# First batch of a block-sparse attention and feed-forward kernel: value products with turned probabilities as 32-column stationary tiles, outputs normalised after the product and then turned, first loads in another order

## The chip, the core and the metric

The kernel runs on one core of a Trainium2 chip. TensorE (PE) multiplies matrices; it holds a stationary operand that is loaded by its own instruction (PEld in the profile) and streams a moving operand through it. VectorE (DVE), ScalarE (ACT) and GpSimd (POOL) do elementwise work, and the DMA queues are fed by the SP and ACT instruction streams. The metric is the device time of one execution, in microseconds (us), lower is better.

## The reference, cut to what matters

```python
# batch 4, heads 8, sequence 768, head size 64; blocks of 32 rows, 24 blocks
scores = q @ k.T / 8
mask = |block_i - block_j| <= 1, or block 0 or 23 on either side, or one of 3 sampled blocks
scores = where(mask, scores, -1e9); scores -= max(scores)
attn = exp(scores); attn = attn / (sum(attn) + 1e-9)
x = (attn @ v)            # laid out as 3072 tokens x 512
out = ((x @ w_a) * (x @ w_b)) @ w_out    # 512 -> 1536 -> 512, float32 results
```

A query block of 32 rows (a "unit" below) reads all 768 keys if it is block 0 or 23 (a dense unit) and 8 blocks, 256 keys, otherwise (a sparse unit).

## The kernel before, in words

The program is written by generators that ask a planner (`Plan`) for time on an engine. The planner holds an assumed duration for every step (`pe(1050, ...)`, `dve(420, ...)`), picks the next step greedily by its assumed start, with a weight times the step's rank added on DVE, SP and the loads, and so fixes the order of the instructions on every engine before anything runs. On the chip each engine then works its list off in order, with semaphore waits between engines. So a change of an assumed duration or of a rank can change the order everywhere.

Work goes by chunks of 256 query rows (8 units), 12 chunks in all. The first batch has the chunks 0, 1 and 2, taken in the order 1, 0, 2: chunk 1 is eight sparse units, chunk 0 is one dense and seven sparse, chunk 2 seven sparse and one dense. Batches 1 to 3 are computed with operands split in two 16-bit parts; the first batch ("plain") is computed in float32, since the splitting machinery is not running yet, and since the three feed-forward weight matrices have to be unpacked and split in the same time (`weights`, lines L751 to L801: load, three DVE passes, an ACT pass for the bound, and the split on ACT and DVE, 36 pieces).

A sparse unit of the first batch goes: POOL collects the keys (`gather_keys`, L603 to L608); PE writes the duplicate mask (L971) and adds the scores (`plain_scores`, L820: four heads, each 32 stationary columns of queries, into four 32-row strips of PSUM); DVE takes the maximum (L986); ACT does exp with the sum (L999) into `sm`; DVE takes the reciprocal (L1006); `plain_norm` multiplies `sm` by it, once for each of two groups of four heads (L924 on DVE or L927 on ACT); `plain_turn` transposes the four 128-column pieces on PE (L940) and copies them from PSUM (L947 or L948) to `pt`; then `values_into` multiplies by the values (L878). There the stationary operand is 128 columns of values (two heads of 64) and the moving operand is 64 columns of `pt` (two heads of 32 queries), so the result `av` comes with head and feature on the partitions, as the feed-forward part wants it. Of the product of two heads by two heads, half is used. When two units are done, `output` writes `xT` in two 16-bit parts from each half of the partitions (`output_half`, L1210 on ACT and L1211 on DVE, 64 partitions by 256, twice).

A dense unit does the same in four quarter steps (two groups of heads, two halves of the keys) with 384 keys each, and has one normalisation and three transposes for each.

`first_products` (L1246) multiplies `xT` by the weights, one of 12 slices of the 1536 at a time, when a chunk's `xT` and that slice's weights are there; `second_products` (L1334 to L1336) does the other matrix. The PSUM ring `ab` (two buffers) serves both L1246 and the transposes L940.

At the start the ACT queue issues the four key loads, then the first value load, a query load, three value loads, a query load, the three small tables (sampled blocks twice, block constants) with the 128x128 identity (`eye`, which borrows a buffer of the ring `hl`), and then the weights. A load is planned on an engine of its own (`LOAD`) though ACT issues it. The mask rows (`mrows`, 8 blocks by 32 equal columns) and the offsets of the sampled blocks are computed on DVE from the small tables. The values are loaded at the start only to find their bound (L532, `v_scale`), which `output` needs; the products read them by their own loads (`gather_values`, L638 to L654, on SP).

Of the kernel before, what the change touches and what calls it, by code (L numbers as in the profile page):

```python
# [9 lines left out]
BF16 = mybir.dt.bfloat16  # L10
# [8 lines left out]
NB = 24  # L19
# [36 lines left out]
W_PE, W_DVE, W_ACT, W_POOL, W_SP = 0, 1, 0, 0, 2  # L56
SLACK = 0
R_NOW, R_P2, R_P1 = -50, 8000, 9000

# [173 lines left out]
def load_way(moved, fn):  # L233

    return [Way("LOAD", 475, fn, moved)]

# [6 lines left out]
def kernel(  # L243
# [96 lines left out]
    v_stored = [Event(NG) for _ in range(B)]  # L340
    q_ready = [Event(3 if cc >= NCH else 2) for cc in range(NC)]
    tables = Event()
    eye_ready = Event()
    eye, eye_used = [None], Event(NB - 2 + 4 * HQ)
    mask_ready = Event()
# [42 lines left out]


    def make_tables():  # L390

        box = work.tile([P, DM], F32, tag="st", name="mbox", bufs=ST_BUFS)
        held = yield from take("st", ST_BUFS)
        row = work.tile([P, DM], F32, tag="st", name="mrow", bufs=ST_BUFS)
        rings.setdefault("hl", Ring(HL_BUFS)).freed.append(eye_used)
        whole = work.tile([P, 2 * HQ * NK // 2], F32, tag="hl", name="eye", bufs=HL_BUFS)
        eye[0] = whole[:, :P]
        held2 = yield from take("st", ST_BUFS)
# [9 lines left out]
        def load():  # L408
            nc.scalar.dma_start(
                one.rearrange("p a b -> p (a b)"),  # L410
                sampled_blocks.bitcast(I32).rearrange("(o a) b -> o (a b)", o=1),
            )
            nc.scalar.dma_start(
                sb.rearrange("p a b -> p (a b)"), sampled_blocks.bitcast(I32)
            )
            nc.scalar.dma_start(cb, c_blocks)
            nc.scalar.dma_start(eye[0], c_eye)

        t = yield [Way("ACT", 300, load, 500)]
        eye_ready.fire(t)  # L420

# [15 lines left out]
        def doubles():  # L437
            nc.vector.tensor_copy(sv[:, 0:5], cb[:, 0:5])
            nc.vector.tensor_scalar(
                sv[:, 5:8], sb[:, :, 0], 0.0, float(NB - 1), ALU.max, ALU.min  # L440
            )
            nc.vector.memset(ident, 0.0)
            nc.vector.memset(mrows, 0.0)
            nc.vector.tensor_copy(ident[:NB], cb[:, 5 : 5 + NB])
            nc.vector.memset(dup, 0.0)
            for s in range(3, 8):
                nc.vector.tensor_scalar(
                    eq[:, :s], sv[:, :s], sv[:, s : s + 1], MASKED, ALU.is_equal, ALU.mult
                )
# [3 lines left out]
            nc.vector.tensor_copy(mrows[:NB], dup.unsqueeze(2).to_broadcast([NB, 8, BLK]))  # L453

# [25 lines left out]
    def keys(b, g):  # L480
        if b == 0:
            t = yield load_way(1000, lambda: nc.scalar.dma_start(plain_keys[:, g], k[0, g]))
            k_ready[0].fire(t)
            if g + 1 < NG:
                plan.start(keys(0, g + 1), -LEAD_K)
            return
# [33 lines left out]
    def values(b, g):  # L520
# [194 lines left out]
    def plain_queries(cc, u0):  # L715

        q_used[cc] = yield from take("QT", QT_BUFS)
        t = work.tile([P, 2, NG, CH], F32, tag="QT", name=f"QZ{cc}", bufs=QT_BUFS)
        QT[cc] = t
        parts_of = [slice(0, D), slice(D, P)]  # L720

        def blank():
            for y in range(2):
                nc.gpsimd.memset(t[parts_of[1 - y], y], 0.0)

        end = yield pool(1800, blank)
# [132 lines left out]
    def values_into(b, i, quads, first, last):  # L859


        if i % 2 == 0 and quads[0][0] == 0 and first:
            av_ev[0] = yield from take("av", 2)
            av_ps[0] = psum.tile([P, NG, 2, 64], F32, tag="av", name=f"av{b}_{i}", bufs=2)
        av = av_ps[0]

        def pair_sums(g, terms):
            cols = slice((g % 2) * 64, (g % 2) * 64 + 64)
            each = []
            for pt, hi, lo, vals in terms:  # L870
                if lo is None:
                    each.append((vals[:, g % 2 * P : g % 2 * P + P], pt, hi))
                    continue
                v0 = g % 2 * 4 * D
# [14 lines left out]

        each = 240 if b == 0 else 180  # L890
        t = yield pe(sum(len(terms) for _, terms in quads) * each + 80, sums)
        if last and quads[-1][0] == HQ - 1:
# [28 lines left out]

    def plain_norm(sm, over, n):
        return [
            Way("DVE", 150 + n * 0.53, lambda: nc.vector.tensor_scalar(  # L924
                sm, sm, over, None, ALU.mult
            )),
            Way("ACT", 290 + n * 0.83, lambda: nc.scalar.activation(  # L927
                sm, sm, AF.Copy, scale=over
            )),
        ]  # L930

    def plain_turn(sm, pt, name, freed):
# [5 lines left out]
        def turns_():  # L938
            for x in range(cols):
                nc.tensor.transpose(ps[:, x], sm[:, x * P : (x + 1) * P], eye[0])  # L940

        t = yield pe(110 * cols, turns_)
        freed.fire(t)
        eye_used.fire(t)
        n = cols * P
# [7 lines left out]
    def attend(b, i):  # L953
# [27 lines left out]

        t = yield pe(1050 if b == 0 else 850, all_scores)
        kg_free[kn].fire(t)
# [20 lines left out]
        if b == 0:  # L1004
# [3 lines left out]
            mine.fire(0)  # L1008
            for hq in range(HQ):
                yield plain_norm(sm[:, hq], den[:, at, hq, 0:1], NK)  # L1010
            mine = yield from turn("pt", b, i)
# [8 lines left out]
                (hq, [  # L1020
                    (pt, 2 * hq + x, None, vg[:, x, hq * 4 * D : (hq + 1) * 4 * D])
                    for x in range(2)
# [54 lines left out]
    def attend_quad(b, i, hq, ends):  # L1077
# [17 lines left out]
        for x in range(2):  # L1095
            t = yield pe(700 if b == 0 else 450, lambda x=x: half_scores(x))
        if hq == 0:
# [63 lines left out]
    def all_values(b, i, hq, x, pt, kept):  # L1161
# [6 lines left out]
        if b == 0:  # L1168
            vg = plain_vg(m).rearrange("p a x -> p (a x)")
            terms = [(pt, y, None, vg[:, y * 4 * D : (y + 1) * 4 * D]) for y in range(3)]  # L1170
        else:
# [14 lines left out]
    def output(b, i, av, read):  # L1186
# [3 lines left out]
        if p >= 2:  # L1190
            yield ffn_done[seq[p - 2]]
        if b == 0:
            yield v_scale[0]
        t0 = i % PER * BLK
        left = Event(2)
        for half in range(2):
# [5 lines left out]
            lo4 = lo.rearrange("p g (i x) -> p g i x", i=2)  # L1202
            plan.start(output_half(cc, half, of, hi4, lo4, left, read), order[b, i] - LEAD_X)
        yield from ()

    def output_half(cc, half, of, hi, lo, left, read):
        s = float(2.0 ** -14)
        if cc < NCH:
            s = scale[half * 64 : half * 64 + 64, at_v : at_v + 1]
        yield act(380, lambda: nc.scalar.activation(hi, of, AF.Copy, scale=s))  # L1210
# [182 lines left out]
def _laid_out(name, a):  # L1393
# [11 lines left out]
    elif name in ("k", "v"):  # L1405

        B, H, S, _ = a.shape
        first = a[0].transpose((0, 2, 1) if name == "k" else (1, 0, 2))
        a = a.reshape(B, H // 2, 2, S // P, P, D)
# [37 lines left out]
```

## Time and profile before

| | |
|---|---|
| median of 3 runs | 929.02 us (922.42 to 936.56) |
| the profiled execution's own time | 930.45 us |
| its span, first to last instruction | 928.7 us |
| busy: PE, DVE, ACT, POOL | 835.5, 549.9, 435.8, 169.3 us |
| mean granted clock of TensorE in it | 0.969 of full speed |

The trace is of the one profiled execution, so sums are made against its 930.45 us. A float32 matmul of the first batch stands in the trace as two records (two passes), a transpose as one. Busy shares are of a stretch; PEclk is the granted clock as a share of 2.4 GHz. First-batch attention runs from about 21 to 262 us of the span.

### The profile page before, as it was taken

What the parts mean: (1) busy time and instruction counts of PE and PEld (TensorE: products, weight loads), DVE (VectorE), ACT (ScalarE), POOL (GpSimd) and SP (SyncE); (2) the same over time, 40 slices, a digit from 0 to 9 for tenths busy, and PEclk for the clock granted to TensorE, in tenths of its full rate; (3) what the DMA queues carried; (4) which work ended last, traced back from release to release, by engine and by line L of the source; (5) the groups of instructions that cost most, each with busy time, mean ns of one, the idle gap of its engine ahead of it and who ended that gap; (6) DMA issues with size and microseconds to landing.
All of it is one profiled execution on the core that took longest, in us unless ns stands there. A gap on an engine that the chain in (4) does not pass through costs nothing.

```text
span 928.7 us, 23488 instructions
## 1 busy us (share of the span) xinstructions
PE 835.5 (90%) x8912; PEld 669.1 (72%) x8912; DVE 549.9 (59%) x1527; ACT 435.8 (47%) x1074; POOL 169.3 (18%) x415
## 2 busy tenths in 40 slices
PE   0788987899998787989999999999989999999998
PEld 0466865678876665777777777778777787788886
DVE  1778898966567665555666665645675625332222
ACT  2455655666546475543465564434655424232222
POOL 3431313112033331100332220001421300000000
PEclk9777997999999998999999999999999999999999
DMA  8655684397577599974686985627755506442000
GB/s 258 211 161 185 185 256 138 123 187 207 141 167 169 136 224 168 191 152 95 161 153 164 225 170 154 144 68 167 164 127 139 115 13 145 94 96 48 24 1 23
DMA packets 173083, 133.48 MB, mean 144 GB/s; under 512 B 116841, under 2 KB 141546, under 8 KB 172394
## 3 DMA queue, kind: packets, MB, share of 16 engines
q1 hardware_dynamic: 161760, 94.15, 45.1%
q10 hardware_dynamic: 11210, 37.82, 13.4%
q8 instruction: 70, 1.15, 0.5%
q14 instruction: 43, 0.35, 0.1%
HBM read 87.89 MB, written 12.58 MB: 108 GB/s over the span
## 4 chain that ended last, share of the span: by engine, by line
PE 52%; DMA 18%; DVE 15%; ACT 6%; SPq 5%; issue 3%; ACTq 0%; POOL 0%; POOLq 0%; DVEq 0%
PE ab L1246 24%; DMA pt<-hl 10%; PE av L878 8%; PE o L1334 5%; PE o L1336 4%; PE o L1335 4%; DMA keysT<-ks 2%; DVE hl L854 2%; PE s L820 2%; ACT sm L999 2%; DVE xT L1211 2%; SPq L652 2%; PE tp L940 2%; DVE hl L850 2%; ACT xT L1210 1%
## 5 line engine op out<-in xcount | busy, mean ns | idle before, releaser
L1246 PE MATMUL ab<-xT,wab 128*128 128x256 f16 x3456 | 407.3, 275 | 3.6 <-DVE a L1281 2.8
L1246 PEld LDWEIGHTS <-wab 128*128 128x128 f16 x3456 | 330.9, 99 | 73.6 <-issue 34.0
L878 PE MATMUL av<-pt,VG 128*128 128x64 f16 (+1 forms) x2464 | 138.0, 212 | 22.1 <-DMA VG<-vd 15.6
L1334 PE MATMUL o<-woh,gh 128*128 128x512 f32 x288 | 126.5, 439 | 10.0 <-ACT gh L1303 8.8
L1281 DVE TENSOR_TENSOR a<-a,ab 128x256 f32<-128x256 f32 x144 | 59.9, 416 | 124.7 <-ACT a L1278 123.7
L1278 ACT ACTIVATE a<-ab,f 128x256 f32<-128x256 f32 x144 | 67.8, 471 | 126.0 <-PE ab L1246 120.7
L1336 PE MATMUL o<-woh,gl 128*128 128x512 f32 x288 | 114.9, 399 | 1.2 <-DVE gl L1306 1.0
L603 POOL COPY KG<-keysT 128x384 int32<-128x384 int32 (+1 forms) x88 | 52.0, 591 | 347.2 <-PE s L829 240.3
L1335 PE MATMUL o<-wol,gh 128*128 128x512 f32 x288 | 113.1, 393 | 0.0
L999 ACT ACTIVATE sm<-s,low,cq 128x256 f32<-128x256 f32 x132 | 73.6, 561 | 65.0 <-DVE hl L854 33.1
L608 POOL COPY KG<-keysT 128x128 int32 (+1 forms) x264 | 91.8, 385 | 40.7 <-POOL KG L603 26.0
L878 PEld LDWEIGHTS <-VG 128*128 128x128 f16 x2016 | 69.3, 98 | 34.7 <-issue 23.5
L1303 ACT CAST gh<-a 128x256 fp32r<-128x256 f32 x132 | 53.2, 403 | 84.9 <-DVE a L1281 83.4
L850 DVE TENSOR_SCALAR hl<-sm,den 128x256 f16<-128x256 f32 (+1 forms) x117 | 43.6, 374 | 66.4 <-DMA pt<-hl 66.3
L854 DVE SCALAR_TENSOR_TENSOR hl<-sm,den,hl 128x256 f16<-128x256 f32 (+1 forms) x156 | 78.8, 513 | 6.2 <-ACT hl L847 4.6
L1306 DVE TENSOR_TENSOR gl<-a,gh 128x256 fp32r<-128x256 f32 x132 | 57.9, 439 | 35.0 <-ACT gh L1303 33.3
L1334 PEld LDWEIGHTS o<-woh,gh 128*128 128x128 f32 x288 | 54.6, 190 | 28.4 <-ACT gh L1303 11.4
L1336 PEld LDWEIGHTS o<-woh,gl 128*128 128x128 f32 x288 | 54.3, 188 | 17.3 <-DVE gl L1306 5.0
L878 PEld LDWEIGHTS av<-pt,VG 128*128 128x128 f32 x448 | 59.9, 213 | 7.5 <-DVE pt L948 2.9
L986 DVE TENSOR_REDUCE low<-s 128x2 f32<-128x512 f32 x88 | 59.9, 681 | 7.6 <-PE s L820 5.6
L971 PE MATMUL s<-mrows,ident 128*32 128x192 bf16 (+1 forms) x352 | 25.1, 274 | 43.6 <-ACT sm L999 21.8
L1335 PEld LDWEIGHTS o<-wol,gh 128*128 128x128 f32 x288 | 54.8, 190 | 6.7
(109 smaller groups left out, 827.6 us busy)
## 6 DMA issues: line engine op xcount, KB each, us to landing
VG<-vd SPq DMA_DIRECT2D x210, 64.0 KB, 2.1
VG<-vd SPq DMA_DIRECT2D x66, 192.0 KB, 2.9
VG<-vd SPq DMA_DIRECT2D x24, 384.0 KB, 3.6
out_dram<-ou SPq DMA_DIRECT2D x24, 256.0 KB, 2.4
VG<-in_v_dram SPq DMA_DIRECT2D x74, 64.0 KB, 2.8
q<-in_q_dram ACTq DMA_DIRECT2D x9, 512.0 KB, 5.2
stage<-in_k_dram ACTq DMA_DIRECT2D x12, 384.0 KB, 4.3
QT<-QT SPq DMA_DIRECT2D x18, 256.0 KB, 3.7
```

The lines of the kernel that those rows point to most:

```text
L608: nc.gpsimd.tensor_copy(to[:, :, (5 + r) * w : (6 + r) * w], of[:, :, bass.ds(at, w)])
L850: Way("DVE", 227 + n * 0.49, lambda: nc.vector.tensor_scalar(hi, sm, over, None, ALU.mult), 0, X_HIGH),
L854: t = yield dve(221 + n * 1.03, lambda: nc.vector.scalar_tensor_tensor(lo, sm, over, hi, ALU.mult, ALU.subtract))
L878: mm(av[:, g, i % 2, :], w, pt[:, y, cols], start=(i % 2 == 0 and g == 0 and first and n == 0), stop=(last and n == len(each) - 1), skip_g ...
L986: yield dve(685, lambda: nc.vector.tensor_reduce(mx, ps, axis=mybir.AxisListType.X, op=ALU.max, negate=True))
L999: t = yield act(750, lambda hq=hq: nc.scalar.activation(sm[:, hq], ps[:, hq], AF.Exp, bias=low[:, at, hq, 0:1], scale=factor_of(b, cc, hq) ...
L1246: mm(ab[:, i, :], wab[:, f, i, part, kt, :], xc[:, kt, a, :], start=(i == 0 and kt == 0 and part + a == 0), stop=(kt == KT - 1 and a == 1) ...
L1278: yield act(470, lambda: nc.scalar.activation(a_sb, ab[:, 0, :], AF.Copy, scale=fb[:, f : f + 1]))
L1281: t = yield dve(420, lambda: nc.vector.tensor_mul(a_sb, a_sb, ab[:, 1, :]))
L1334: mm(po, gh[:, js], woh[:, f, :], start=(f == 0), stop=False)
L1335: mm(po, gh[:, js], wol[:, f, :], start=False, stop=False)
L1336: mm(po, gl[:, js], woh[:, f, :], start=False, stop=(f == NF - 1))
```

## The change

For the first batch, the value product has the turned probabilities of one head as stationary operand (32 columns) and the head's 64 value columns as moving operand; four heads go to four 32-row strips of PSUM, as the scores do. The probabilities are turned without being normalised. After each pair of units the product is multiplied by the reciprocal sums on DVE (`xs`), turned back by two PE transposes into a buffer of the ring `ab`, and the two parts of `xT` are written from all 128 partitions at once. Heads are grouped by even and odd for that, with the value layout, the key indices and the query indices arranged to fit.

At the start the tables and the query loads go through SP, the four key loads are started together with ranks ahead of everything else on ACT, the identity has its own buffer and load, the bound's value loads get a later rank, and the value gathers of the first batch wait for the keys. Loads are planned on ACT. `mrows` is held as 8 columns, and the mask matmul reads each of them 32 times (step 0). The planner's assumed durations of the first batch's PE steps change.

```diff
+PLAIN_S, PLAIN_T, PLAIN_AV = 430, 215, 240
...
-    return [Way("LOAD", 475, fn, moved)]
+    return [Way("ACT", 475, fn, moved)]
...
-    mrows = const.tile([P, 8, BLK], BF16, name="mrows")
+    mrows = const.tile([P, 8], BF16, name="mrows")
+    eye = const.tile([P, P], F32, name="eye")
...
+    def load_eye():
+        t = yield load_way(300, lambda: nc.scalar.dma_start(eye, c_eye))
+        eye_ready.fire(t)
...
-        t = yield [Way("ACT", 300, load, 500)]
-        eye_ready.fire(t)
+        yield [Way("SP", 1300, load, 250, 1)]
+        plan.start(load_eye(), -20)
...
-            plan.start(values(b, g + 1), order[b, 0] - LEAD_V)
+            plan.start(values(b, g + 1), order[b, 0] - (LEAD_V if b else 1))
...
-        if b > 0:
-            yield v_stored[b]
+        yield v_stored[b] if b > 0 else k_ready[0]
...
-            end = yield load_way(700, lambda y=y: nc.scalar.dma_start(
+            end = yield sp(650, 700, lambda y=y: nc.sync.dma_start(
...
-            g, y = divmod(4 * hq + h, 2)
             mm(
-                to[h * BLK : (h + 1) * BLK], QT[cc][:, y, g, r : r + BLK], rhs(g),
+                to[h * BLK : (h + 1) * BLK], QT[cc][:, hq, h, r : r + BLK], rhs(h),
...
+        def plain_sums():
+            for hq, terms in quads:
+                for n, (pt, y, vals) in enumerate(terms):
+                    for h in range(4):
+                        mm(
+                            av[h * BLK : (h + 1) * BLK, i % 2, hq, :],
+                            pt[:, y, h * BLK : (h + 1) * BLK], vals[:, h * D : (h + 1) * D],
+                            start=(i % 2 == 0 and hq == 0 and first and n == 0),
+                            stop=(last and n == len(terms) - 1), skip_group_check=True,
+                        )
...
-    def plain_norm(sm, over, n):
...
-                    mrows[:, lo:].rearrange("p s x -> p (s x)").unsqueeze(1).to_broadcast(
-                        [P, HQ, NK - lo * BLK]
+                    mrows[:, lo:].unsqueeze(1).unsqueeze(3).to_broadcast(
+                        [P, HQ, 8 - lo, BLK]
...
-            for hq in range(HQ):
-                yield plain_norm(sm[:, hq], den[:, at, hq, 0:1], NK)
...
-                yield plain_norm(sms[x], d1, HALF)
...
+    def plain_output(i, av, read, to, cc):
+
+        at = order[0, i] % LATE
+        held = yield from take("hl", HL_BUFS)
+        xs = work.tile([P, 2, HQ, D], F32, tag="hl", name=f"xs{i}", bufs=HL_BUFS)
+        over = den[:, at : at + 2, :, 0].unsqueeze(3).to_broadcast([P, 2, HQ, D])
+        t = yield dve(418, lambda: nc.vector.tensor_mul(xs, av, over))
+        read.fire(t)
+        freed = yield from take("ab", 2)
+        ps = psum.tile([P, NG, 2, BLK], F32, tag="ab", name=f"tx{i}", bufs=2)
+
+        def turns_():
+            for x in range(2):
+                nc.tensor.transpose(
+                    ps[:, :, x], xs[:, x].rearrange("p a d -> p (a d)"), eye
+                )
+
+        t = yield pe(2 * PLAIN_T, turns_)
+        held.fire(t)
+        yield v_scale[0]
+        s = scale[:, at_v : at_v + 1]
+        of = ps.rearrange("p g i x -> p g (i x)")
+        hi, lo = to[:, :, 0], to[:, :, 1]
+        yield act(470, lambda: nc.scalar.activation(hi, of, AF.Copy, scale=s))
+        t = yield dve(420, lambda: nc.vector.scalar_tensor_tensor(
+            lo, of, s, hi, ALU.mult, ALU.subtract
+        ))
+        freed.fire(t)
...
-        plan.start(keys(0, 0), -LEAD_K)
-        plan.start(queries(seq[0]), -LEAD_Q)
-        plan.start(make_tables(), 0)
-        plan.start(values(0, 0), -LEAD_V)
+        for g in range(NG):
+            plan.start(keys(0, g), -29 + g)
+        plan.start(queries(seq[0]), -30)
+        plan.start(make_tables(), -40)
+        plan.start(values(0, 0), -1)
```

## Rows read from the trace of the kernel before

**Rows 1.** Busy us by stretch: PE, PEld, DVE, ACT, POOL, PEclk, DMA share, GB/s:

```profile
0.00:20.00 20.00, 0.00 (x0) 0.10 (x1) 2.33 (x17) 5.12 (x10) 7.64 (x21) 1.00 0.85 257
20.00:80.00 60.00, 44.79 (x351) 32.31 (x354) 44.23 (x122) 27.04 (x73) 18.71 (x38) 0.74 0.64 199
80.00:200.00 120.00, 105.05 (x915) 82.80 (x907) 102.96 (x279) 71.78 (x174) 27.98 (x58) 0.93 0.58 172
200.00:265.00 65.00, 64.59 (x597) 53.12 (x594) 38.12 (x99) 35.06 (x80) 9.16 (x22) 1.00 0.67 174
```

**Rows 2.** The chain that ended last, 20 to 80 and 80 to 200 us:

```profile
by line: PE av L878 31.0%; PE s L820 15.2%; PE tp L940 11.5%; DMA stage<-in_moe_w_b_dram 10.9%; ACT xT L1210 5.3%; DVE xT L1211 4.9%; DVE wab L770 3.7%; DVE wab L773 3.3%; ACT sm L999 2.4%; PE s L971 2.3%; DVE low L986 2.2%; ACT sm L927 1.9
...
by line: PE ab L1246 15.1%; PE av L878 13.6%; DMA keysT<-ks 8.3%; PE s L820 5.7%; DVE w L770 4.7%; DVE w L773 4.5%; PE tp L940 3.9%; DVE wab L795 3.0%; ACT xT L1210 2.8%; issue 2.8%; DMA VG<-in_v_dram 2.6%; DVE low L986 2.5%; DVE w L767 2.4
```

**Rows 3.** Timeline of the first 32 us: start, duration, what:

```profile
8.73 0.50 POOL L603 COPY KG<-keysT 128x384 f32<-128x384 f32 x1 [4.07 <-DMA keysT<-in_k_dram]
...
11.06 0.69 ACTq L409 DMA_DIRECT2D mrow<-in_sampled_blocks_dram  x1
...
15.60 0.18 DVE L423 TENSOR_SCALAR mrow<-mrow 1x72 f32<-1x72 int32 x1 [14.64 <-DMA mrow<-in_sampled_blocks_dram]
...
17.18 0.77 POOL L608 COPY KG<-keysT 128x128 f32 x3 [7.47 <-issue]
...
18.24 0.19 DVE L438 COPY mbox<-mbox 24x5 f32<-24x5 f32 x1
...
21.51 0.35 PE L971 MATMUL s<-mrows,ident 128*32 128x192 bf16 x4 [21.51 <-DVE mrows L453]
...
23.69 0.43 DVE L767 TENSOR_SCALAR wab<-stage 128x512 int32<-128x512 int32 x1 [1.90 <-DMA stage<-in_moe_w_b_dram]
```

**Rows 4.** Busy time by stretch of the value products (L878) alone, PE and PEld:

```profile
20.00:80.00 60.00, 21.13 (x128) 20.39 (x128) 0.74 0.64 199
80.00:200.00 120.00, 23.14 (x176) 22.43 (x176) 0.93 0.58 172
200.00:265.00 65.00, 17.96 (x162) 17.75 (x162) 1.00 0.67 174
```

**Rows 5.** PE timeline: start, duration, what:

```profile
35.42 3.68 PE L878 MATMUL av<-pt,VG 128*128 128x64 f32 x16
38.89 1.91 PE L940 MATMUL tp<-eye,sm 128*128 128x128 f32 x8
...
103.53 0.49 PE L940 MATMUL tp<-eye,sm 128*128 128x128 f32 x3
103.95 0.27 PE L971 MATMUL s<-mrows,ident 128*32 128x192 bf16 x4
104.04 1.04 PE L820 MATMUL s<-KG,QZ 128*32 128x256 f32 x16
105.01 1.55 PE L878 MATMUL av<-pt,VG 128*128 128x64 f32 x12
...
108.23 1.89 PE L878 MATMUL av<-pt,VG 128*128 128x64 f32 x16
109.96 0.61 PE L940 MATMUL tp<-eye,sm 128*128 128x128 f32 x4
110.49 0.27 PE L971 MATMUL s<-mrows,ident 128*32 128x192 bf16 x4
```

**Rows 6.** The chain that ended last, 120 to 310 us, a 16-bit score group:

```profile
282.95 0.44 PE s L829 x16
```

**Rows 7.** Groups by form: busy us and mean ns, then idle before:

```profile
L1281 DVE TENSOR_TENSOR a<-a,ab 128x256 f32<-128x256 f32 x144 | 59.9, 416 | 124.7 <-ACT a L1278 123.7
...
L1211 DVE SCALAR_TENSOR_TENSOR xT<-av,scale,xT 64x256 f16<-64x256 f32 x24 | 11.6, 482 | 19.3 <-ACT xT L1210 19.0
```

**Rows 8.** Busy time by stretch of the normalisations on DVE (L924):

```profile
20.00:80.00 60.00, 5.06 (x14) 0.74 0.64 199
80.00:200.00 120.00, 5.17 (x15) 0.93 0.58 172
```

More of the change, by code (lines that the diff above doesn't have):

```diff
@@ L340 @@
     v_stored = [Event(NG) for _ in range(B)]
-    q_ready = [Event(3 if cc >= NCH else 2) for cc in range(NC)]
+    q_ready = [Event(3) for _ in range(NC)]
     tables = Event()
     eye_ready = Event()
-    eye, eye_used = [None], Event(NB - 2 + 4 * HQ)
     mask_ready = Event()
@@ L394, in make_tables @@
         row = work.tile([P, DM], F32, tag="st", name="mrow", bufs=ST_BUFS)
-        rings.setdefault("hl", Ring(HL_BUFS)).freed.append(eye_used)
-        whole = work.tile([P, 2 * HQ * NK // 2], F32, tag="hl", name="eye", bufs=HL_BUFS)
-        eye[0] = whole[:, :P]
         held2 = yield from take("st", ST_BUFS)
@@ L408, in load @@
         def load():
-            nc.scalar.dma_start(
+            nc.sync.dma_start(
                 one.rearrange("p a b -> p (a b)"),
@@ L452, in doubles @@
                 )
-            nc.vector.tensor_copy(mrows[:NB], dup.unsqueeze(2).to_broadcast([NB, 8, BLK]))
+            nc.vector.tensor_copy(mrows[:NB], dup)
         t = yield dve(2300, doubles)
@@ L483, in keys @@
             k_ready[0].fire(t)
-            if g + 1 < NG:
-                plan.start(keys(0, g + 1), -LEAD_K)
             return
@@ L722, in blank, with memsets @@
         def blank():
-            for y in range(2):
-                nc.gpsimd.memset(t[parts_of[1 - y], y], 0.0)
-        end = yield pool(1800, blank)
+            def memsets():
+                for y in range(2):
+                    nc.gpsimd.memset(t[parts_of[1 - y], y], 0.0)
+            end = yield pool(1900, memsets)
+            q_ready[cc].fire(end)
+        plan.start(blank(), u0 - LEAD_Q)
         for y in range(2):
-            end = yield load_way(700, lambda y=y: nc.scalar.dma_start(
+            end = yield sp(650, 700, lambda y=y: nc.sync.dma_start(
                 t[parts_of[y], y], q[0, cc, :, y * NG : (y + 1) * NG]
@@ L863, in values_into @@
             av_ev[0] = yield from take("av", 2)
-            av_ps[0] = psum.tile([P, NG, 2, 64], F32, tag="av", name=f"av{b}_{i}", bufs=2)
+            shape = [P, 2, HQ, D] if b == 0 else [P, NG, 2, 64]
+            av_ps[0] = psum.tile(shape, F32, tag="av", name=f"av{b}_{i}", bufs=2)
         av = av_ps[0]
+        def plain_sums():
[8 more added lines that the diff above has]
+                        )
         def pair_sums(g, terms):
@@ L870, in pair_sums @@
             for pt, hi, lo, vals in terms:
-                if lo is None:
-                    each.append((vals[:, g % 2 * P : g % 2 * P + P], pt, hi))
-                    continue
                 v0 = g % 2 * 4 * D
@@ L888, in sums @@
                     pair_sums(g, terms)
-        each = 240 if b == 0 else 180
-        t = yield pe(sum(len(terms) for _, terms in quads) * each + 80, sums)
+        n_terms = sum(len(terms) for _, terms in quads)
+        if b == 0:
+            t = yield pe(n_terms * PLAIN_AV + 80, plain_sums)
+        else:
+            t = yield pe(n_terms * 180 + 80, sums)
         if last and quads[-1][0] == HQ - 1:
@@ L920, in factor_of @@
         return D ** -0.5 if b == 0 else cq[:, cc, hq : hq + 1]
-    def plain_norm(sm, over, n):
[L923 to L930, printed above, removed]
     def plain_turn(sm, pt, name, freed):
@@ L939, in turns_ @@
             for x in range(cols):
-                nc.tensor.transpose(ps[:, x], sm[:, x * P : (x + 1) * P], eye[0])
-        t = yield pe(110 * cols, turns_)
+                nc.tensor.transpose(ps[:, x], sm[:, x * P : (x + 1) * P], eye)
+        t = yield pe(PLAIN_T * cols, turns_)
         freed.fire(t)
-        eye_used.fire(t)
         n = cols * P
@@ L980, in all_scores @@
                 heads(ps[:, hq], cc, i, hq, lambda h: kg[:, h], False)
-        t = yield pe(1050 if b == 0 else 850, all_scores)
+        t = yield pe(180 + 2 * PLAIN_S if b == 0 else 850, all_scores)
         kg_free[kn].fire(t)
@@ L1020, in attend @@
                 (hq, [
-                    (pt, 2 * hq + x, None, vg[:, x, hq * 4 * D : (hq + 1) * 4 * D])
+                    (pt, 2 * hq + x, vg[:, x, hq * 4 * D : (hq + 1) * 4 * D])
                     for x in range(2)
@@ L1095, in attend_quad @@
         for x in range(2):
-            t = yield pe(700 if b == 0 else 450, lambda x=x: half_scores(x))
+            t = yield pe(1.5 * PLAIN_S if b == 0 else 450, lambda x=x: half_scores(x))
         if hq == 0:
@@ L1169, in all_values @@
             vg = plain_vg(m).rearrange("p a x -> p (a x)")
-            terms = [(pt, y, None, vg[:, y * 4 * D : (y + 1) * 4 * D]) for y in range(3)]
+            terms = [(pt, y, vg[:, y * 4 * D : (y + 1) * 4 * D]) for y in range(3)]
         else:
@@ L1191, in output @@
             yield ffn_done[seq[p - 2]]
+        t0 = i % PER * BLK
         if b == 0:
-            yield v_scale[0]
-        t0 = i % PER * BLK
+            yield from plain_output(i, av, read, xT[p % 2][:, :, :, t0 : t0 + 2 * BLK], cc)
+            return
         left = Event(2)
@@ L1202, in output, with output_half @@
             lo4 = lo.rearrange("p g (i x) -> p g i x", i=2)
-            plan.start(output_half(cc, half, of, hi4, lo4, left, read), order[b, i] - LEAD_X)
+            plan.start(output_half(cc, of, hi4, lo4, left, read), order[b, i] - LEAD_X)
         yield from ()
-    def output_half(cc, half, of, hi, lo, left, read):
+    def plain_output(i, av, read, to, cc):
[23 more added lines that the diff above has]
+        freed.fire(t)
+        x_ready[cc].fire(t)
+        x_ready[cc].fire(t)
+    def output_half(cc, of, hi, lo, left, read):
         s = float(2.0 ** -14)
-        if cc < NCH:
-            s = scale[half * 64 : half * 64 + 64, at_v : at_v + 1]
         yield act(380, lambda: nc.scalar.activation(hi, of, AF.Copy, scale=s))
@@ L1405, in _laid_out @@
     elif name in ("k", "v"):
-        B, H, S, _ = a.shape
-        first = a[0].transpose((0, 2, 1) if name == "k" else (1, 0, 2))
+        B, H, S, D = a.shape
+        first = a[0].transpose(0, 2, 1)
+        if name == "v":
+            first = a[0].reshape(H // 2, 2, S, D).transpose(2, 1, 0, 3)
         a = a.reshape(B, H // 2, 2, S // P, P, D)
```

5 lines of the change are left out of this document (2 added, 3 removed).

## The prediction

> **What bounds the kernel now.** I read the busy time by stretch first, then the chain that ended last in those stretches, then the timeline of the first microseconds, then the groups that the change touches. The reader is to see four stages up to 265 us, each with another limit, and nothing of the change behind them but the mask matmuls.
>
> Until 20 us PE does nothing: DMA is 85% busy, and the first matmul starts at 21.51, released by the mask rows [rows 1, 3]. The keys are there at 8.73, but the offset table is issued at 11.06, behind the value loads, and lands at 15.60; the mask rows follow on DVE from 18.24 to 21.51. So the small tables, not the large loads, end that wait.
>
> From 20 to 80 us PE is 45 of 60 us busy at a granted clock of 0.74, a mixture of the levels 1.2 and 2.4 GHz [rows 1]. Of the chain there, value products, scores and transposes have 31.0, 15.2 and 11.5% [rows 2]: PE at its low clock sets the end. From 80 to 200 us PE and DVE are both 86 to 88% busy and the chain goes back and forth; the feed-forward slices wait for weights, and the weights come at the pace of DVE. From 200 to 265 us PE is 64.6 of 65 us busy at full clock: there every PE microsecond counts [rows 1].
>
> **The value products.** A sparse unit's product is 16 records. At full clock it takes 109.96 - 108.23 = 1.73 us, 108 ns each; at the low level 38.89 - 35.42 = 3.47 us [rows 5]. That is for 64 moving columns, while the scores stream 256 columns with 32 stationary ones in at most (105.01 - 103.95) / 16 = 66 ns a record, with the mask's four in it [rows 5]. So four 32-row strips do run side by side, and the product of now is held by its 128-column stationary loads, not by its columns. The new product has twice the records (32 a unit). Its cost isn't in the trace. The lower end is by columns: 66 x 64 / 256 x 32 = 0.53 us. The upper end is no gain, 1.73. The nearest row is the 16-bit scores, also 32 stationary columns, 16 records in 0.44 us [rows 6]: 27.5 ns each, so 32 take 0.88 us. I take that, as the only row of matmuls that follow each other so closely on 32-column strips; it saves 49%.
>
> The Trainium skill has a rule against reading more out of the columns: in TensorE: Matmul & The Clock Gate, section "Wait — 56ns, not 53.3ns?", starts of matmuls never come closer than about 25 ns, however few columns. That would make 0.80 us of the unit, an estimate, some 2 us less in the whole sum, and 0.53 impossible; no row here shows records closer than 27.5 ns.
>
> The value products are busy 21.1, 23.1 and about 16 us in the three stretches (18.0 in the last, of which 18 records belong to the second batch and take about 2 us) [rows 4]. 49% of these is 10.4, 11.3 and 7.8 us.
>
> **What is added on PE.** Two transposes a pair of units, 12 pairs, so 8 in each stretch, for each chunk has four pairs. A transpose takes 1.91 / 8 = 0.24 us at the low clock and (110.49 - 109.96) / 4 = 0.13 us at full [rows 5]: 1.9, 1.1 and 1.1 us. The array also changes between 128 and 32 columns where a product stood between wide matmuls. Three transposes from 103.53 at 0.13 end at 103.92, and the narrow mask starts at 103.95 [rows 5]: 0.03 us a change. I count 30 products with two changes as 0.3 us in each stretch more or less; with 0.1 us a change the sum would lose 4 us more. The skill's TensorEngine Tiling (Array Packing), section "Key Properties", says that a change of the tiling mode drains the engine; the row shows hardly any of that.
>
> PE is left with 8.2, 9.8 and 6.4 us less in the three stretches.
>
> **DVE and ACT.** The normalisations go: 5.1 and 5.2 us of DVE in the second and third stage [rows 8], and some on ACT. The outputs go from two 64-partition operations of 482 ns to one of 128 partitions by the same 256 columns, which saves 0.48 us a pair, and `xs` adds one like the product with a PSUM operand, 416 ns [rows 7]: net nothing much. So DVE has 5.3 us less in each of these stages. PE no longer waits for a normalisation ahead of a transpose, but for `xs` ahead of the new ones; I cost that exchange at nothing, since four products or scores can be put between, and at 12 x 0.42 = 5 us if nothing stands there. Queued behind that wait on PE are the feed-forward slices, and the `ab` buffer that they share.
>
> **The front.** Table loads at about 1 us instead of 11.06 land 4.5 us later, near 5.5, and the mask rows are ready some 3.3 us of DVE work later, near 9 [rows 3]. The keys now share the queues with 0.5 MB of queries: at 257 GB/s [rows 1] that puts 8.73 back to about 10.7; the gather takes 1 us and the three sampled copies 0.77 [rows 3]. The first score comes near 12.5 instead of 21.5: 9 us. The weights gain less. Their first pair is worked on from 23.69 [rows 3], and the same bytes go ahead of them; only the 15% of the 20 us in which DMA was idle [rows 1] can be won, 3 us. I take 6. The queries on SP stand ahead of the value gathers there; before the first score that costs nothing, as both are needed. A late query load of chunk 2 could stand behind a gather that waits for a buffer; chunk 2 is far enough off.
>
> The identity's own buffer, the planning of the loads on ACT and the planner's new durations cost nothing by themselves; they change the order of instructions, for which I allow 5 us to either side. The mask columns read 32 times are the one edit that reaches all batches: 88 units x 0.27 us [rows 5]. I take 0 for it, as the columns streamed are as many as before; if reading one column again and again were slow by half, it would cost 12 us, and a gain I exclude, since the count of columns stays.
>
> **The sum.** Front 6; 20 to 80 us: between DVE's 5.3 and PE's 8.2, so 6, as PE has more than half of the chain but the first feed-forward slices then wait for weights; 80 to 200 us: DVE's 5.3, as the weights set the pace; 200 to 265 us: PE's 6.4. Together 23.7 us. 930.45 - 23.7 = 906.8 for the profiled execution; the median of the runs is 1.4 lower than that execution, so **905 us**.
>
> **Rivals.** (1) PE sets the end everywhere, and the weights keep up: 9 + 8.2 + 9.8 + 6.4 = 33.4, so 896 us. For it: the 58% of the chain from 20 to 80 us [rows 2]; against it: DVE's 86% between 80 and 200 us. (2) The weights decide, and the second batch doesn't start sooner than its keys allow, so that PE's saving after 200 us becomes idle time: 3 + 5.3 + 5.3 = 13.6, so 915 us. For it: the transposed keys hold 8.3% of the chain before 200 us [rows 2]; against it: PE is never idle from 200 to 265 us. (3) The change doesn't do what it says: strips whose stationary operand changes with every record don't overlap, a unit stays at 1.73 us, and the transposes come on top: 6 - 2.2 + 5.3 - 1.4 = 7.7, so 921 us. Against it stand the scores. (4) Slower than before: the lighter PE stream between 80 and 200 us falls to the 1.2 GHz level as it did from 20 to 80 us, where the granted clock is 0.74 though PE was 75% busy [rows 1]. The work there is 105 x 0.93 - 9.8 = 88 us at full clock; if half of it runs at the low level, 44 us come on top, and the time is 949 us; it is slower than before from 23.7 / 88 = 27% on. Against it: the feed-forward slices still fill that stretch.
>
> **How the numbers follow.** The forecast has 0.5, rivals 1 to 4 have 0.13, 0.2, 0.1 and 0.07. A measurement of this kernel tells about 2% from no change; 2% under 929.02 is 910.4. The forecast's own range, 898 to 914 by the 5 us for the order and 2 to 4 for the unit's cost, lies for four fifths under that: 0.4, with rival 1 and a little of rival 2 makes 0.56 for faster. Slower is rival 4 alone, 0.07; the rest is 0.37. The range from 893 to 922 takes in the forecast and rivals 1 to 3.
>
> **What would show it.** In the changed kernel's profile: the first score near 12 us; the value product of a sparse unit near 0.9 us at full clock, and 62 us of it in all near 30; the last weight piece of DVE some 15 us earlier; PE full from there until the second batch starts; a granted clock between 80 and 200 us not below 0.9. The prediction is wrong if the product keeps 1.7 us, if that clock falls, if the mask matmuls take longer than 0.27 us, or if the second batch begins about 20 us earlier and the time after it grows.

## The result and the profile after

The changed kernel took 897.45 us (895.73 to 898.63, four runs) beside 925.8 us of the kernel before (922.42 to 936.56, four runs): a ratio of 0.9704, with a 95% interval of 0.9651 to 0.9757. Ratios, the base of each group of experiments and the table of the last four leave out slow runs, which are those more than 1.5% above the fastest run of their kernel. The forecast was 905 us, in a range of 893 to 922. The profiled execution has a span of 895.2 us, 33.5 less than before. PE's busy time in it is 32.8 us less (802.7 for 835.5), and its idle time 0.7 (92.5 for 93.2). The mean granted clock is 0.971 for 0.969, so over the whole execution no higher clock explains the gain.

Busy time by stretch in the changed kernel (columns as in [rows 1]):

```profile
0.00:20.00 20.00, 4.60 (x48) 2.20 (x52) 5.69 (x26) 4.38 (x10) 9.16 (x25) 1.00 0.79 218
20.00:80.00 60.00, 47.62 (x749) 30.91 (x741) 55.58 (x155) 35.20 (x98) 24.55 (x51) 0.91 0.85 273
80.00:200.00 120.00, 101.78 (x1216) 72.97 (x1215) 101.94 (x268) 75.49 (x179) 29.77 (x58) 0.93 0.73 207
200.00:265.00 65.00, 51.00 (x743) 39.89 (x743) 43.41 (x125) 33.16 (x88) 19.95 (x49) 0.93 0.73 161
```

The reader is to see the second row beside [rows 1]: DVE went from 44 to 56 of 60 us, and the granted clock from 0.74 to 0.91. The last stretch isn't the first batch any more; the second one begins at 193.5 us.

The timeline of the first 32 us of the changed kernel (beside [rows 3]):

```profile
0.74 0.35 SPq L411 DMA_DIRECT2D mrow<-in_sampled_blocks_dram  x1
...
7.75 0.35 PE L973 MATMUL s<-mrows,ident 128*32 128x192 bf16 x4 [7.75 <-DVE mrows L454]
...
13.43 0.50 POOL L602 COPY KG<-keysT 128x384 f32<-128x384 f32 x1 [8.76 <-DMA wab<-in_v_dram]
...
15.48 1.93 PE L821 MATMUL s<-KG,QZ 128*32 128x256 f32 x16 [7.38 <-POOL KG L607]
...
19.38 0.45 ACTq L753 DMA_DIRECT2D stage<-in_moe_w_a_dram  x1
...
26.83 0.45 DVE L769 TENSOR_SCALAR wab<-stage 128x512 int32<-128x512 int32 x1
```

The mask rows are ready at 7.75 us (forecast: 9), but the gather of the keys starts only at 13.43 (forecast: 10.7), so the first score comes at 15.48 and not at 12.5: 6.0 us earlier than before, not 9. The table no longer ends that wait; the copy of the keys does, and the row puts its wait down to a load of values. The weights gained nothing at the start: their first pair is worked on from 26.83 us, 3.1 us later than at 23.69 [rows 3], where the forecast had 3 us earlier.

PE timeline of the changed kernel, a product at the low clock, then one at full clock, then two of the new transposes (beside [rows 5]):

```profile
101.60 0.86 PE L873 MATMUL av<-VG,pt 128*32 128x64 f32 x32 [1.20 <-ACT pt L949]
102.39 0.80 PE L1363 MATMUL o<-woh,gh 128*128 128x512 f32 x1
...
119.11 0.67 PE L873 MATMUL av<-VG,pt 128*32 128x64 f32 x32 [0.70 <-DVE pt L950]
119.59 0.28 PE L973 MATMUL s<-mrows,ident 128*32 128x192 bf16 x4
...
123.79 0.44 PE L1219 MATMUL tx<-eye,xs 128*128 128x128 f32 x2 [3.06 <-DVE xs L1212]
```

The product takes 119.59 - 119.11 = 0.48 us at full clock and 0.79 at the low one, against 1.73 and 3.47 [rows 5]. The last row shows the wait that the change adds: PE stood 3.06 us for `xs`. By stretch the product alone (beside [rows 4]), and the groups by form of what the change adds and of the mask (beside [rows 7]):

```profile
20.00:80.00 60.00, 8.26 (x352) 6.56 (x352) 0.91 0.85 273
80.00:200.00 120.00, 10.31 (x472) 7.80 (x472) 0.93 0.73 207
200.00:265.00 65.00, 1.63 (x72) 1.14 (x72) 0.93 0.73 161
```

```profile
L973 PE MATMUL s<-mrows,ident 128*32 128x192 bf16 x320 | 22.0, 263 | 32.6 <-ACT sm L1001 24.7 <-DVE mrows L454 7.8
...
L1230 DVE SCALAR_TENSOR_TENSOR xT<-tx,scale,xT 128x256 f16<-128x256 f32 x12 | 5.7, 475 | 2.5 <-ACT xT L1229 2.4
...
L1219 PE MATMUL tx<-eye,xs 128*128 128x128 f32 x24 | 5.4, 308 | 7.8 <-DVE xs L1212 7.8
L1212 DVE TENSOR_TENSOR xs<-av,den 128x256 f32<-128x256 f32 x12 | 4.9, 410 | 0.0
```

The group of the product in the kernel before (PE) and in the changed one:

```profile
L878 PE MATMUL av<-pt,VG 128*128 128x64 f32 x448 | 61.5, 297 | 1.9 <-DVE pt L948 1.4 <-ACT pt L947 0.5
```

```profile
L873 PE MATMUL av<-VG,pt 128*32 128x64 f32 x896 | 20.2, 226 | 7.8 <-DMA VG<-in_v_dram 3.6 <-DVE pt L950 2.4 <-ACT pt L949 1.8
```

The product's busy time went from 61.5 to 20.2 us, the new transposes cost 5.4 us and 7.8 us of waiting for `xs`, and the mask with its columns read again and again keeps its 263 ns.

Two milestones came much earlier. The last weight piece on DVE starts at 156.8 us, 34 us earlier than in the kernel before; in the view of one line (minimum, median and maximum ns, first and last start) the row of the kernel before, then that of the changed one:

```profile
L795 DVE SCALAR_TENSOR_TENSOR wab<-w,scale,wab x8: 734/746/769, 145.5 to 191.0; 128x512 f16<-128x512 f32 x8
```

```profile
L797 DVE SCALAR_TENSOR_TENSOR wab<-w,scale,wab x8: 732/739/776, 117.0 to 156.8; 128x512 f16<-128x512 f32 x8
```

Between the first pair of weights and the last piece DVE, with PE and the others beside it (columns as in [rows 1]), was busy as follows in the kernel before, then in the changed one:

```profile
23.70:191.80 168.10, 139.45 (x1147) 107.44 (x1137) 140.94 (x373) 94.47 (x234) 45.01 (x90) 0.86 0.57 178
```

```profile
26.80:157.60 130.80, 105.99 (x1398) 73.47 (x1402) 127.52 (x341) 80.50 (x205) 43.81 (x79) 0.91 0.72 223
```

The stretch is 37.3 us shorter. Of that 13.4 us are work of DVE, and 23.9 are idle time of DVE: it was 84% busy there before, and is 97% busy now.

And the second batch's first score comes at 193.5 us, 51 us earlier than at 244.4. But the time from there to the end grew. Busy time around that moment in the kernel before, all engines and then the first feed-forward products alone (L1246; L1275 in the changed kernel):

```profile
244.40:928.70 684.30, 641.67 (x7282) 518.11 (x7281) 372.20 (x1042) 303.52 (x755) 107.08 (x281) 0.99 0.57 127
...
20.00:244.40 224.40, 61.61 (x504) 50.23 (x504) 0.89 0.63 183
```

The same in the changed kernel:

```profile
193.50:895.20 701.70, 654.55 (x7465) 529.47 (x7453) 379.59 (x1047) 309.54 (x766) 111.66 (x281) 0.98 0.57 127
...
20.00:193.50 173.50, 51.12 (x408) 41.02 (x408) 0.92 0.77 230
```

17.4 of the 51 us are paid after it: 12.9 us of PE work, among it the 96 feed-forward records that hadn't been done by then (504 before, 408 now), and 4.5 us of idle time. A batch that starts earlier is no gain by itself where PE has left other work behind.

### The profile page after: what moved, and what is told of

The parts are those of the page before. It is cut to its first block, busy times and chain, and to the rows that moved or that the text cites. A ratio compares the mean times of both kernels' runs of the same rounds, so it can differ in the third digit from the quotient of the medians.

```text
span 895.2 us, 24316 instructions
## 1 busy us (share of the span) xinstructions
PE 802.7 (90%) x9384; PEld 631.1 (70%) x9384; DVE 539.4 (60%) x1488; ACT 421.9 (47%) x1049; POOL 175.1 (20%) x415
## 4 chain that ended last, share of the span: by engine, by line
PE 41%; DMA 14%; DVE 9%; ACT 5%; SPq 4%; issue 2%; POOL 0%; ACTq 0%; POOLq 0%; DVEq 0%
PE ab L1275 23%; DMA pt<-hl 11%; PE o L1363 4%; PE o L1365 4%; PE o L1364 4%; PE av L888 4%; DVE hl L855 3%; DMA VG<-vd 2%; ACT sm L1001 2%; PE s L830 2%; DVE hl L851 1%; SPq L650 1%; SPq L572 1%; ACT xT L1239 1%; DVE low L988 1%
## 5 line engine op out<-in xcount | busy, mean ns | idle before, releaser
L1275 PE MATMUL ab<-xT,wab 128*128 128x256 f16 x3456 | 407.3, 275 | 2.7 <-DVE a L1310 2.7
L1275 PEld LDWEIGHTS <-wab 128*128 128x128 f16 x3456 | 330.8, 99 | 72.3 <-issue 33.2
L1363 PE MATMUL o<-woh,gh 128*128 128x512 f32 x288 | 128.3, 445 | 7.0 <-ACT gh L1332 4.8
L602 POOL COPY KG<-keysT 128x384 int32<-128x384 int32 (+1 forms) x88 | 54.7, 622 | 318.9 <-PE s L830 252.7
L1001 ACT ACTIVATE sm<-s,low,cq 128x256 f32<-128x256 f32 x132 | 73.7, 561 | 70.8 <-DVE low L994 29.5
L607 POOL COPY KG<-keysT 128x128 int32 (+1 forms) x264 | 94.6, 395 | 39.5 <-POOL KG L602 26.7
L888 PE MATMUL av<-pt,VG 128*128 128x64 f16 x2016 | 77.4, 195 | 14.6 <-DMA VG<-vd 7.7
L1240 DVE SCALAR_TENSOR_TENSOR xT<-av,xT 64x256 f16<-64x256 f32 x72 | 30.4, 422 | 43.4 <-ACT xT L1239 42.5
```

The lines of the kernel that those rows point to most:

```text
L607: nc.gpsimd.tensor_copy(to[:, :, (5 + r) * w : (6 + r) * w], of[:, :, bass.ds(at, w)])
L888: mm(av[:, g, i % 2, :], w, pt[:, y, cols], start=(i % 2 == 0 and g == 0 and first and n == 0), stop=(last and n == len(each) - 1), skip_g ...
L1001: t = yield act(750, lambda hq=hq: nc.scalar.activation(sm[:, hq], ps[:, hq], AF.Exp, bias=low[:, at, hq, 0:1], scale=factor_of(b, cc, hq) ...
L1275: mm(ab[:, i, :], wab[:, f, i, part, kt, :], xc[:, kt, a, :], start=(i == 0 and kt == 0 and part + a == 0), stop=(kt == KT - 1 and a == 1) ...
L1363: mm(po, gh[:, js], woh[:, f, :], start=(f == 0), stop=False)
```

## The experiments

Theory A: TensorE's time for the product makes the gain. Theory B: the planner's new numbers and the planning of the loads make a better order. Theory C: the earlier start makes it. Theory D came with the seventh run: VectorE and the waits of the first 200 us set the time, and TensorE's saving counts in part. Medians; ratios are against the kernel before on the same chip (medians of 928.6 us for the first four, 927.3 for the next four, 923.6 for the last four).

**e1_same_strip.**

```diff
-                for n, (pt, y, vals) in enumerate(terms):
-                    for h in range(4):
+                for h in range(4):
+                    for n, (pt, y, vals) in enumerate(terms):
```

> The changed kernel with the loops of the value product exchanged, so that the products of one head, which go to the same 32-row strip of PSUM, follow each other; the order of all other instructions and the planner's durations are the same. Theory A, strips side by side: the gain is TensorE time, and the product is cheap only because four strips run at once. Then a sparse unit's 32 records go from 0.48 us to about 1.0 to 1.7 us at full clock, and the time from 897 us to 912 to 930 us. Theory B, order: the planner's new durations and the earlier loads made a better order, which is unchanged here: 897 to 902 us. Theory C, front: the earlier start made it: 897 to 902 us.

896.74 us, 0.9644 (0.9599 to 0.9689). The edit was too weak to tell: with only two matmuls of one strip in a row the product's busy time went from 20.2 to 26.1 us. That 6 us of TensorE time weren't seen in the end is all that follows.

**e2_front_only.** The kernel before with

```diff
-    return [Way("LOAD", 475, fn, moved)]
+    return [Way("ACT", 475, fn, moved)]
...
-        t = yield [Way("ACT", 300, load, 500)]
+        yield [Way("SP", 1300, load, 250, 1)]
...
-            end = yield load_way(700, lambda y=y: nc.scalar.dma_start(
+            end = yield sp(650, 700, lambda y=y: nc.sync.dma_start(
...
+        for g in range(NG):
+            plan.start(keys(0, g), -29 + g)
```

> The kernel before with the front of the change alone: tables and queries on SP, keys together, identity in its own buffer, later loads of the values' bound, loads planned on ACT, mask columns read with step 0. Theory A: 6 us of TensorE idle time at the start go and the rest stays, 917 to 924 us. Theory C: 897 to 908 us. Theory B, as far as the planning of the loads on ACT is the better order: 900 to 915 us.

929.09 us, 1.002 (0.9988 to 1.0053): the front alone is worth nothing that shows in this interval. Theory C falls as the whole cause, and so does the forecast's 6 us as a part that stands by itself. The start is earlier there too, first score 16.2 us, last weight piece 172.8, second batch 228.9 us; the busy time from there on is the row to read:

```profile
228.90:927.60 698.70, 653.53 (x7372) 529.89 (x7371) 375.46 (x1041) 310.24 (x770) 108.26 (x281) 0.99 0.55 127
```

PE's work is the same in all (837.3 us busy against 835.5), and what didn't get done before 228.9 us is done behind it: 11.9 us of PE more than from 244.4 us on in the kernel before. The granted clock from 20 to 80 us is 0.89 in this run, against 0.74 before (0.90 against 0.93 from 80 to 200 us), so the higher clock of that stretch gains nothing by itself either.

**e3_products_only.** The changed kernel with the reverse of the edit above (loads on `LOAD`, tables, queries and identity on ACT, old ranks).

> The changed kernel with the front of the kernel before (tables, queries and identity on ACT behind the value loads, loads planned on an engine of their own), the value products, outputs and durations of the change kept. Theory A: 900 to 908 us, the loss being the 6 us of the start. Theory C: 915 to 925 us.

909.9 us, 0.9798 (0.9739 to 0.9857): the front is worth 12 us beside the new products. PE is busy 801.7 us, like the changed kernel's 802.7, but idle 105.9 us against 92.5. The new products take 34 us off PE, and without the front 13 of them turn into idle time.

**e4_norms_back.**

```diff
+    def times_one(sm, n):
+        return dve(150 + n * 0.53, lambda: nc.vector.tensor_scalar(
+            sm, sm, 1.0, None, ALU.mult
+        ))
...
+            for hq in range(HQ):
+                yield times_one(sm[:, hq], NK)
...
+                yield times_one(sms[x], HALF)
```

> The changed kernel with the normalisations of the probabilities put back on VectorE as multiplications by one, in the places of the kernel before: 60 operations of 350 to 420 ns, some 22 us of VectorE. Theory A with VectorE setting the pace from 40 to 160 us, as its full busy time there says: 8 to 20 us more, 905 to 917 us. If only TensorE's busy time counts: 897 to 902 us.

906.49 us, 0.9755 (0.9717 to 0.9793): 9 us more. They were 52 operations, not 60:

```profile
L936 DVE TENSOR_SCALAR sm<-sm 128x256 f32<-128x256 f32 x44 | 13.3, 310 | 0.0
...
L936 DVE TENSOR_SCALAR sm<-sm 128x384 f32<-128x384 f32 x8 | 2.8, 348 | 0.0
```

16 us of DVE cost 9, so VectorE's time does count there. VectorE's busy time as a whole rose by 11.0 us only, from 539.4 to 550.4: it has 49 instructions more and ACT 3, so the planner also moved other steps.

**e5_before_true_product.**

```diff
-        each = 240 if b == 0 else 180
+        each = 430 if b == 0 else 180
```

> The kernel before with one number of the planner changed: a term of the first batch's value product counts 430 ns in place of 240, which is what it takes at full clock (1.73 us for four). No instruction is added or removed, only the order moves. Theory B, order: the outputs that VectorE waited 19 us for stood too early in its queue because the planner took the product for shorter than it is; with the right number much of the gain comes, 900 to 915 us. Theory A, TensorE time: 922 to 932 us.

932.64 us, 1.0063 (1.0021 to 1.0105): if anything worse, and DVE waits longer for the output step than the 19.0 us before. Waits of DVE from 20 to 265 us, the kernel before and then this run (us in total, times, longest):

```profile
DVE xT L1211 <- ACT xT L1210: 19.0, 11, 3.4
```

```profile
DVE xT L1211 <- ACT xT L1210: 23.8, 10, 4.7
```

So that wait doesn't come from this wrong number of the planner. In the changed kernel the like wait is 2.4 us (L1230 above).

**e6_after_true_times.**

```diff
-PLAIN_S, PLAIN_T, PLAIN_AV = 430, 215, 240
+PLAIN_S, PLAIN_T, PLAIN_AV = 430, 130, 120
```

> The changed kernel with the planner's numbers set to what the trace shows at full clock: 120 ns a term of the product (0.48 us for four) in place of 240, 130 ns a transpose in place of 215. Theory B: some us less, 888 to 895 us. Theory A: 892 to 902 us, no difference beyond the spread.

896.58 us, 0.9678 (0.9615 to 0.9742): no difference from the changed kernel. Theory B is left with the planning of the loads, and with those of the planner's numbers that e5 and e6 didn't touch.

**e7_strip_by_strip.**

```diff
-            for hq, terms in quads:
-                for n, (pt, y, vals) in enumerate(terms):
-                    for h in range(4):
+            for h in range(4):
+                for hq, terms in quads:
+                    for n, (pt, y, vals) in enumerate(terms):
```

> The changed kernel with the head as the outermost loop of the value product, so that a sparse unit's eight records for one 32-row strip follow each other; the order of everything else is kept. If records of one strip can't overlap, a sparse unit goes from 0.48 us to 1.2 to 1.7 us at full clock and the product's busy time from 20 us to 45 to 60. Theory A: 20 to 30 us of the gain go, 915 to 928 us. Theories B and C: 895 to 902 us.

902.65 us, 0.975 (0.9685 to 0.9814). PE timeline and group of this run:

```profile
123.52 1.23 PE L873 MATMUL av<-VG,pt 128*32 128x64 f32 x29 [2.25 <-DVE pt L950]
```

```profile
L873 PE MATMUL av<-VG,pt 128*32 128x64 f32 x896 | 41.0, 229 | 14.7 <-DMA VG<-in_v_dram 9.4 <-DVE pt L950 3.5 <-ACT pt L949 1.8
```

The same records in another order take twice the time, 41.0 us for 20.2: the product is cheap because neighbours go to different strips. Rival 3 is refuted by that and by the 0.48 us. But 20.8 us in this group cost about 5 us in the end (runs of 897.4 to 907.1 beside 894.4 to 899.9, which overlap), a quarter; theory A's 20 to 30 did not come. Part of the rest came back at a higher granted clock: 0.97 from 20 to 80 us, against 0.91 in the changed kernel, with PE 80% busy against 79%. PE's busy time as a whole rose by 10.2 us only (812.9 against 802.7). Why the clock is higher with the longer products, the runs don't settle.

**e8_loads_own_engine.**

```diff
-    return [Way("ACT", 475, fn, moved)]
+    return [Way("LOAD", 475, fn, moved)]
```

> The changed kernel with the loads planned on an engine of their own, as before; all other parts of the front stay new. If the earlier tables make the 12 us that the front was worth beside the new products: 895 to 901 us. If the planning of the loads on ACT makes them: 904 to 912 us.

901.92 us, 0.9742 (0.9667 to 0.9817), with runs from 895.8 to 906.6: between the two expectations, and not told apart. The planning of the loads may be worth some 4 of the 12 us.

**e9_product_thrice, e10_thrice_norms, e11_thrice_norms_front, e12_after_again.** Each adds one part of the old work to the one before it; the base is the changed kernel, e12. The edit of e9 is shown, e10 adds that of e4, and e11 that of e3.

```diff
+                    for w in range(3):
...
-                            start=(i % 2 == 0 and hq == 0 and first and n == 0),
-                            stop=(last and n == len(terms) - 1), skip_group_check=True,
+                                start=(i % 2 == 0 and hq == 0 and first and n == 0 and w == 0),
+                                stop=(last and n == len(terms) - 1 and w == 2),
```

> The changed kernel with every value product of the first batch done three times into the same sum (so that the first batch's x is three times too large): 96 records a sparse unit, 1.44 us at full clock, 60 us of TensorE in all, as much as before the change. The order and the planner's numbers are unchanged. Theory A, TensorE time makes the gain: 925 to 935 us. Theory D, the time is set by VectorE and by waits in the first 200 us, and TensorE's saving is worth about a quarter there, as the strip-by-strip run showed (20.8 us for 5): 905 to 912 us.

> The same (the first batch's x three times too large) with the normalisations put back as multiplications by one on VectorE besides. If the parts add: 8 to 10 us more than with the product thrice alone, 914 to 921 us under theory D. If either hides behind the other: within 4 us of the product thrice alone.

> The same (the first batch's x three times too large) with the front of the kernel before besides, so that of the change only the outputs' way, the order and the planner's numbers remain. If the parts add: 12 us more, 925 to 933 us, the time before, and the outputs' way is worth nothing. If the front is worth nothing where TensorE has its old work, as it was alone: 914 to 921 us.

> The changed kernel itself, beside the three others on the same chip: 895 to 900 us by all theories.

| run | median us | runs | step | PE busy, idle of its profile |
|---|---|---|---|---|
| e12, the changed kernel | 896.31 | 894.4 to 899.9 | | 802.7, 93.5 |
| e9, product thrice | 908.87 | 908.8 to 914.0 | +12.6 | 821.0, 86.0 |
| e10, and the norms | 909.54 | 907.4 to 915.5 | +0.7 | 822.5, 83.1 |
| e11, and the old front | 926.80 | 920.3 to 931.4 | +17.3 | 822.5, 101.2 |
| the kernel before | 923.61 | 915.2 to 927.9 | | 835.5, 93.2 |

Idle is the span less the busy time; the last row's are those of the trace of the kernel before that all other readings use. The median of e9 is of three runs; its fourth took 922.8 us. The intervals of e9 and e10 (0.9706 to 1.006 and 0.9758 to 1.0011) are wide, but their runs don't meet those of e12. The group of the product in e9:

```profile
L874 PE MATMUL av<-VG,pt 128*32 128x64 f32 x2688 | 48.3, 226 | 13.2 <-DMA VG<-in_v_dram 4.7 <-issue 4.6 <-DVE pt L952 2.0
```

28.1 us more in this group cost 13 us; PE's busy time as a whole rose by 18.3 us, again at a higher granted clock (0.97 from 20 to 80 us, against 0.91). Theory A's 925 to 935 us did not come. Beside that the 16 us of DVE cost next to nothing, though alone they cost 9: the two hide behind each other. With the old front on top the time is that of the kernel before, 1.0032 (0.9983 to 1.0082). So in this order these three parts make up the whole gain. It is no exact return to the old work: the tripled product of e9 is still some 13 us of PE short of the old one (48.3 against 61.5), and the outputs keep their new way. What those two are worth against each other, and against the new order, isn't shown.

## Why the prediction was right, step by step

**The stages.** That PE and DVE set the end in turns is borne out: with the product cheaper DVE is 93% busy from 20 to 80 us, the norms cost 9 us when put back, and the product's time on PE counts for a quarter (e7) to almost a half (e9). Which of the two set it in which stage isn't shown. The sum took 6 and 5.3 us for the two stages up to 200 us, near the smaller of the two savings, and that was too little: DVE's last weight piece came 34 us earlier. What it left out is DVE's idle time. Its own row shows 19.0 us of DVE waiting ahead of the outputs [rows 7], and it costed the outputs by their busy time alone, at nothing. The wait is 2.4 us in the changed kernel, and 11.9 of the 23.9 us of DVE idle time that went before the last weight piece were this wait. The front doesn't remove it (18.0 us in e2), the new products and outputs do (2.8 us in e3). Rival 1, PE everywhere (896 us), comes out at the measured time, but by luck: it wanted 9 us of the first score, which gained 6, and PE's whole saving in every stage, which e7 and e9 deny.

**The product's unit** is the term that was mis-sized most: 0.88 us taken, 0.48 measured, even below the 0.53 that stood as the lower end, and a saving of some 40 us of busy time for 29.5. The nearest row, the 16-bit scores at 27.5 ns a record, was 256 columns wide and so no bound for 64. Nor was it the closest row: in [rows 5] four mask records stand between 103.95 and 104.04 us, 22.5 ns each. The Trainium skill's floor of about 25 ns between starts (TensorE: Matmul & The Clock Gate, section "Wait — 56ns, not 53.3ns?") doesn't hold for these strips: 32 records in 0.48 us are 15 ns each on average, and the measurement decides.

**The transposes** cost 5.4 us of busy time for 4.1, **`xs`** 410 ns for 416, the outputs 475 for 482, the mask nothing. The exchange of one wait for another that was costed at nothing: PE waits 7.8 us for `xs`, which is past the 5 us set against a missing cover; before, it waited 4.5 and 2.6 us for the normalisations ahead of the transposes (L940) by the view of waits, so that the exchange was about even.

**The front** was taken as 6 us by itself, with the first score at 12.5 us. The score came at 15.5, the weights were worked on 3.1 us later and not 3 earlier, and the 6 us were no term of a sum: nothing alone (e2), 12 beside the new products (e3), 17 beside the old amount of work in the new order (e11).

**The weights' end** was put 15 us earlier and came 34 us earlier, and the second batch 51. This looks like a far larger gain than 24 us, but the time after it grew, by 17.4 us. The forecast had named just that as a sign that it is wrong (the second batch about 20 us earlier, and the time after it longer), and by this sign it was wrong about the last stage. PE was 91% busy from the last weight piece to the second batch, not full. The step that failed is the last of the sum: from 200 to 265 us I counted PE's own saving, as if the first batch still ran there. Its last output starts at 217.0 us, and what PE saved before showed as feed-forward work left for later. The two errors, stages ahead too small and nothing paid back, partly cancel, so that the total came within 8 us of the measured time partly by luck.

**Rival 4**, a lower clock from 80 to 200 us, didn't come: 0.93 as before. From 20 to 80 us the clock rose to 0.91 with PE 79% busy, against 0.74 with 75%.

What stays open: why the front alone gives nothing in the old order, and how much of a change in PE's work comes back through the granted clock. The way of the outputs and the new order couldn't be taken apart further, since the planner writes another order for each; and how much of the front's 12 us is the planning of the loads wasn't settled by e8.

## What to carry to other kernels

Where two engines take turns at setting the end, put each old cost back alone and then together: here 9 us (the norms) and 13 us (the product) alone were 13 together. A milestone that comes 51 us earlier is to be read with the work left behind it, by the busy time of the bounding engine on both sides. For small products, measure the stationary load, the moving columns and the order apart. With the same 64 moving columns a unit took 1.73 us at full clock behind 128-column loads, 1.23 behind twice as many 32-column loads strip after strip (the row of e7, with 29 of the 32 records), and 0.48 with four strips in turn, 3.6 times less than before.

## What was not expected of the hardware

Float32 records with 32 stationary and 64 moving columns, in turn over four strips of PSUM, start 15 ns apart on average at full clock. With two matmuls of one strip in a row the product's busy time is 26.1 us for 20.2, with a strip's whole run in a row 41.0. The Trainium skill's TensorEngine Tiling (Array Packing), section "Key Properties", has different tiles work in parallel; the three orders agree, and show that the order of the instructions decides how much of it is had.
